# Channel mix: both squares of every pair on ScalarE, and other buffers for the last three stores of stage one

## The chip, the cores and the metric

The kernel runs on one core of one Trainium2 chip. The metric is the device time of one execution in microseconds; the time before is 2052.75 us, the median of 3 runs (2052.17 to 2054.95).

## What is computed

Three layers in a row on x of 4 x 3072 x 256 numbers (fp32). The second one is where the change lies; its `k * k` is what the change moves.

```python
def _attn_ref(x, w_r, w_i, b_r, b_i):            # a Fourier layer
    X = np.fft.rfft(x, axis=1)
    Yr = X.real @ w_r - X.imag @ w_i + b_r
    Yi = X.real @ w_i + X.imag @ w_r + b_i
    ...                                          # soft threshold of Yr and Yi at 0.01
    return np.fft.irfft(Yr + 1j * Yi, n=x.shape[1], axis=1)

def _moe_ref(x, mu_k, mu_r, w_k, w_v, w_r):      # the channel mix
    x_prev = ...                                 # x one step earlier
    xk = mu_k * x + (1.0 - mu_k) * x_prev
    xr = mu_r * x + (1.0 - mu_r) * x_prev
    k = np.maximum(xk @ w_k, 0.0)                # 256 -> 1024
    v = k * k @ w_v                              # 1024 -> 256
    return 1.0 / (1.0 + np.exp(-(xr @ w_r))) * v

def _moe2_ref(x, w_in, w_out):                   # 256 -> 2048 -> 256
    h = x @ w_in
    return h * np.tanh(softplus(h)) @ w_out
```

## The kernel before

Every fp32 operand of a matmul is split in two: a part rounded to the matmul's input type (high, `h` at the end of a name) and the rest (low, `l`). A product is three matmuls: high x high, high x low, low x high. `split` (lines 70 to 77) makes both parts: ScalarE casts, VectorE subtracts.

*Stage one*, to 329 us, is the forward transform, the mixing with `w_r` and `w_i`, and the first half of the inverse transform, in 48 units `u`. `load_A` brings a unit from DRAM into tag `A` (four buffers, called the operand ring here), `is1_ev` (lines 392 to 397) copies a result from PSUM into tag `Cs` (two buffers) with ScalarE and stores it to DRAM.

*The channel mix*, 329 to 1022 us, goes over 32 sweeps `t` of 384 columns, in a loop whose body is written out by hand: engines execute in the order in which the code issues. TensorE's order in a sweep is, for the pairs `P = 4t` to `4t + 3` (`i2` from 0 to 3): k of this pair (`emit_k`, line 745, 12 matmuls), v of the pair two before (`emit_v`, line 783, 12 matmuls), and then in pair 0 the second half of the next sweep's inverse transform (`is2`, line 466, 8 matmuls into tile `pp`), in pair 1 the gate (`emit_r`, line 722, 12 matmuls into `pp`), in pair 3 the first half of the transform for the sweep after. `pp` has one PSUM buffer for all three, v has one, k has two.

`k_ev` handles a pair's k: ScalarE's relu into `kr`, then the split for the transform's xk or xr (`then`), then the square, as `kh` and `kl` (two buffers each). Even pairs square twice on ScalarE (lines 768 and 769, rounded and whole) and subtract on VectorE (770). Odd pairs square on VectorE (765), cast on ScalarE (76) and subtract on VectorE (77).

Others that the steps name: `is2_ev` (472 to 485) empties `pp` into `yT`: ScalarE copies to `ya`, VectorE adds. `v_ev` (788 to 792) multiplies the gate with v on VectorE and so frees v's buffer; it is issued in pair 2, behind the `kl` of pair 1. `r_ev` is the gate's sigmoid. `bg` puts decoding steps of the next layer's weights in between (VectorE, lines 117 to 136, and a split). When a sweep is the first of a batch, four more matmuls come (line 440).

*The last layer*, from 1022 us, uses neither.

Of the kernel before, what the change touches and what calls it, by code (L numbers as in the profile page):

```python
# [8 lines left out]
F32 = mybir.dt.float32  # L9
# [8 lines left out]
B, S, D, FK, FF = 4, 3072, 256, 1024, 2048  # L18
N1, N2 = 96, 32
NG = 12  # L20
NU = B * NG
# [8 lines left out]
def kernel(  # L30
# [40 lines left out]
    def split(src, hi, lo, lo_eng=None, hi_eng=None):  # L71

        if hi_eng is nc.vector:
            nc.vector.tensor_copy(out=hi, in_=src)
        else:
            nc.scalar.copy(out=hi, in_=src)  # L76
        (lo_eng or nc.vector).tensor_tensor(out=lo, in0=src, in1=hi, op=ALU.subtract)  # L77
# [77 lines left out]
    p1p = p1.__enter__()  # L155
# [133 lines left out]
    def gview(scr, g):  # L289

        return scr.rearrange("s n d -> (s n) d")[256 * g:256 * (g + 1)].rearrange("(e p) d -> p e d", e=2)
# [100 lines left out]
    def is1_ev(u):  # L392
        b, g = divmod(u, NG)
        p = i1_t.pop(u)
        st = p1p.tile([128, 2, D], F32, tag="Cs", name="Cs", bufs=2)
        nc.scalar.copy(out=st, in_=p)
        nc.sync.dma_start(out=gview(scr2[b], g), in_=st)

# [203 lines left out]
    for u in range(NU + 3):  # L602
# [21 lines left out]
        if u > 2:  # L624
            is1_ev(u - 3)
# [128 lines left out]
    def k_ev(P, then):  # L754
        p = kp_t.pop(P)
        v = p[:, :, 0:TA]
        kr = pap.tile([128, 2, TA], F32, tag="kf", name="kr", bufs=2)
        nc.scalar.activation(out=kr, in_=v, func=AF.Relu)
        if then:
            then()  # L760
        kh = pap.tile([128, 2, TA], F32R, tag="kh", name="kh", bufs=2)
        kl = pap.tile([128, 2, TA], F32R, tag="kl", name="kl", bufs=2)
        if P % 2:

            nc.vector.scalar_tensor_tensor(out=kr, in0=v, scalar=0.0, in1=kr, op0=ALU.max, op1=ALU.mult)  # L765
            split(kr, kh, kl)
        else:
            nc.scalar.activation(out=kh, in_=kr, func=AF.Square)
            nc.scalar.activation(out=kr, in_=kr, func=AF.Square)
            nc.vector.tensor_tensor(out=kl, in0=kr, in1=kh, op=ALU.subtract)  # L770
        kk_t[P] = (kh, kl)
# [27 lines left out]
    for t in range(NA + 1):  # L799
# [5 lines left out]
        for i2 in range(4):  # L805
            P = 4 * t + i2
# [52 lines left out]
            if live:  # L859
                k_ev(P, then)  # L860
# [285 lines left out]
```

## Time and profile before

| | |
|---|---|
| median of 3 runs | 2052.75 us |
| the profiled execution, its span | 2050.79 us, 2049.0 us |
| TensorE busy | 1994.8 us, 97% of the span |
| VectorE, ScalarE, GpSimd busy | 1590.5, 1094.4, 29.6 us |
| stage one, 0 to 329 us: TensorE, VectorE, ScalarE busy | 304.3, 281.6, 195.5 us |
| channel mix, 329 to 1022 us: the same | 676.0, 518.9, 427.8 us |
| last layer, 1022 to 2049 us: the same | 1014.6, 790.0, 471.1 us |
| granted TensorE clock in the three stages | 0.94, 1.00, 1.00 |

Where TensorE is busy 97% of the time, the time to be had lies in its gaps, and a gap is read from the wait that ends it. Durations below are of the one profiled execution.

### The profile page before, as it was taken

To read this page: it belongs to the slowest core of one execution; us is meant where nothing else is said; L and a number is where in the kernel's file an instruction comes from. 1 tells how busy PE (TensorE), PEld (TensorE's weight loads), DVE (VectorE), ACT (ScalarE), POOL (GpSimd) and SP (SyncE) were. 2 spreads that over 40 slices of the span, in tenths; PEclk is the share of its full clock that TensorE was granted. 3 is DMA by queue.
4 is the path that set the end of the run, shared out by engine and by line. 5 is a ranking of instruction groups with operands and counts; after the bars stand their busy time and mean duration, and the time that the engine had idled before them with its cause. 6 is when DMAs were issued, how large, how long until landed. Compare 5 with 4: busy or idle time off the path is not lost.

```text
span 2049.0 us, 33355 instructions
## 1 busy us (share of the span) xinstructions
PE 1994.8 (97%) x13284; PEld 1896.1 (93%) x13284; DVE 1590.5 (78%) x2545; ACT 1094.4 (53%) x1635; POOL 29.6 (1%) x48
## 2 busy tenths in 40 slices
PE   6999998999999999999999999999999999999998
PEld 5999998999999999999979999999999999999997
DVE  5899997777777777777578777777778777787775
ACT  5666555666666666666544444444444444444443
POOL 1000000000000000000000000000000000000000
PEclk6999999999999999999999999999999999999999
DMA  8566632111211212111000000000100001010000
GB/s 254 164 190 205 182 118 75 60 55 59 65 48 57 69 48 67 59 55 48 23 32 31 22 26 27 25 29 21 32 22 29 25 21 32 22 32 21 22 11 21
DMA packets 71499, 123.17 MB, mean 60 GB/s; under 512 B 6192, under 2 KB 48432, under 8 KB 71344
## 3 DMA queue, kind: packets, MB, share of 16 engines
q1 hardware_dynamic: 66864, 105.31, 17.5%
q0 software_dynamic: 4480, 15.73, 2.0%
q8 instruction: 105, 1.72, 0.3%
q14 instruction: 50, 0.41, 0.1%
HBM read 70.69 MB, written 50.33 MB: 59 GB/s over the span
## 4 chain that ended last, share of the span: by engine, by line
PE 76%; DVE 14%; ACT 5%; issue 3%; DMA 2%; SPq 0%; ACTq 0%; DVEq 0%; POOLq 0%
PE h L970 19%; PE o L1018 17%; PE o L1019 9%; PE vp L783 8%; PE kp L745 7%; PE mxp L361 5%; PE p L970 3%; PE s2p L315 2%; PE pp L722 2%; PE pp L466 1%; DVE kl L770 1%; PE s1p L274 1%; DVE kr L765 1%; ACT kh L76 1%; DVE Dl L77 1%
## 5 line engine op out<-in xcount | busy, mean ns | idle before, releaser
L1018 PE MATMUL o<-WO,gh 128*128 128x512 f32 x1536 | 563.4, 395 | 0.0
L1019 PE MATMUL o<-WO,gl 128*128 128x256 f32 x1536 | 431.2, 281 | 0.0
L970 PE MATMUL h<-xS,WS 128*128 128x256 f32 x2208 | 351.9, 282 | 0.0
L1018 PEld LDWEIGHTS o<-WO,gh 128*128 128x128 f32 x1536 | 289.8, 189 | 43.3
L983 ACT COPY p1s<-p 128x256 f32<-128x256 f32 x184 | 68.5, 372 | 478.5 <-PE p L970 477.5
L970 PEld LDWEIGHTS h<-xS,WS 128*128 128x128 f32 x2208 | 300.6, 189 | 16.1
L1019 PEld LDWEIGHTS o<-WO,gl 128*128 128x128 f32 x1536 | 290.4, 189 | 0.2
L745 PE MATMUL kp<-xk,WK 128*128 128x384 f32 x1536 | 290.6, 337 | 0.0
L783 PE MATMUL vp<-kh,WV 128*128 128x384 f32 x1024 | 283.8, 338 | 6.3 <-DVE r L791 6.0
L745 PEld LDWEIGHTS kp<-xk,WK 128*128 128x128 f32 x1536 | 266.6, 188 | 0.1
L973 DVE TENSOR_TENSOR C<-h,p1s 128x512 f32<-128x512 f32 x184 | 127.0, 690 | 163.9 <-PE h L970 163.9
L955 DVE TENSOR_TENSOR gl<-g,gh 128x1024 fp32r<-128x1024 f32 x184 | 223.5, 1215 | 2.1 <-ACT g L952 2.1
L951 ACT ACTIVATE gh<-C 128x1024 fp32r<-128x1024 f32 x184 | 195.7, 1064 | 10.8 <-DVE C L973 10.8
L783 PEld LDWEIGHTS vp<-kh,WV 128*128 128x128 f32 x1024 | 186.4, 188 | 12.8 <-DVE r L791 12.7
L952 ACT ACTIVATE g<-C 128x1024 f32<-128x1024 f32 x184 | 193.0, 1049 | 0.0
L970 PE MATMUL h<-xS,WI 128*128 128x256 f32 x1104 | 190.2, 281 | 0.0
L973 DVE TENSOR_TENSOR C<-h,wu 128x512 f32<-128x512 f32 x368 | 187.3, 550 | 1.8 <-PE h L970 1.8
L783 PE MATMUL vp<-kl,WV 128*128 128x384 f32 x512 | 171.7, 335 | 0.0
L970 PEld LDWEIGHTS h<-xS,WI 128*128 128x128 f32 x1104 | 156.1, 189 | 0.0
L973 DVE TENSOR_TENSOR wu<-h,C 128x512 f32<-128x512 f32 x184 | 126.5, 687 | 37.5 <-PE h L970 33.6
L361 PE MATMUL mxp<-WX,Xh 128*128 128x256 f32 x752 | 138.7, 285 | 0.0
L76 ACT CAST kh<-kr 128x768 fp32r<-128x768 f32 x64 | 53.4, 835 | 154.0 <-DVE kr L765 152.7
(153 smaller groups left out, 3206.1 us busy)
## 6 DMA issues: line engine op xcount, KB each, us to landing
xs<-in_x_dram SPq DMA_DIRECT2D x32, 384.0 KB
A<-scr SPq DMA_DIRECT2D x48, 256.0 KB
scr<-Cs SPq DMA_DIRECT2D x48, 256.0 KB
D<-scr SPq DMA_DIRECT2D x32, 384.0 KB
x2d<-r POOLq DMA_DIRECT2D x32, 384.0 KB, 3.5
x<-x2d SPq DMA_DIRECT2D x24, 512.0 KB
out_dram<-ob SPq DMA_DIRECT2D x96, 128.0 KB
scr<-st SPq DMA_DIRECT2D x24, 384.0 KB
```

The source lines that it names most:

```text
L76: nc.scalar.copy(out=hi, in_=src)
L361: nc.tensor.matmul(out=p[:, e, :], lhsT=a, rhs=WX[:, dh, c, w, :], start=(i == 0), stop=(i == 11))
L745: nc.tensor.matmul(out=p[:, m, 0:TA], lhsT=WK[:, dh, w, f * 128:(f + 1) * 128], rhs=hl[:, v, dh, :], start=(i == 0), stop=(i == 5),)
L783: nc.tensor.matmul(out=p[:, o, 0:TA], lhsT=WV[:, f, w, o * 128:(o + 1) * 128], rhs=v[:, m, :], start=(f == 0 and i == 0), stop=(f == 7 and ...
L951: nc.scalar.activation(out=gh, in_=c, func=AF.Mish)
L952: nc.scalar.activation(out=g, in_=c, func=AF.Mish)
L955: nc.vector.tensor_tensor(out=gl, in0=g, in1=gh, op=ALU.subtract)
L970: nc.tensor.matmul(out=out, lhsT=a(l), rhs=xS[:, v, b, :], start=(n == 0), stop=(n == 2))
L973: nc.vector.tensor_tensor(out=out, in0=x0, in1=x1, op=ALU.add)
L983: nc.scalar.copy(out=p1s, in_=p1)
L1018: nc.tensor.matmul(out=o[m], lhsT=gh[:, m2, ms], rhs=WO[:, f], start=(f == 0), stop=False)
L1019: nc.tensor.matmul(out=o[m][:, 0, :], lhsT=gl[:, m2, ms], rhs=WO[:, f, 0, :], start=False, stop=(f == 15))
```

## The change

Odd pairs take the way of even ones: both squares on ScalarE. And the units 45, 46 and 47 of stage one copy their result into buffers of tag `A` instead of `Cs`.

```diff
     def is1_ev(u):
         b, g = divmod(u, NG)
         p = i1_t.pop(u)
-        st = p1p.tile([128, 2, D], F32, tag="Cs", name="Cs", bufs=2)
+        tag, n = ("Cs", 2) if u < NU - 3 else ("A", 4)
+        st = p1p.tile([128, 2, D], F32, tag=tag, name="Cs", bufs=n)
         nc.scalar.copy(out=st, in_=p)
         nc.sync.dma_start(out=gview(scr2[b], g), in_=st)
...
         kh = pap.tile([128, 2, TA], F32R, tag="kh", name="kh", bufs=2)
         kl = pap.tile([128, 2, TA], F32R, tag="kl", name="kl", bufs=2)
-        if P % 2:
+        if False:
 
             nc.vector.scalar_tensor_tensor(out=kr, in0=v, scalar=0.0, in1=kr, op0=ALU.max, op1=ALU.mult)
             split(kr, kh, kl)
```

The order on TensorE, GpSimd and the DMA queues is the same as before (lines behind 395 move on by one). ScalarE at the end of pair 3 and in pair 0 of a sweep (place A of the prediction), before:

```order
L76 CAST xr<-xf 128x768 [waits DVE_49]
L76 CAST kh<-kr 128x768 [waits DVE_49,PE_49]
L476 COPY yT<-yT 128x3x32 x2
L479 COPY ya<-pp 128x384 [waits PE_49]
L758 ACTIVATE kr<-kp 128x768 [waits PE_49,Activation_49]
L768 ACTIVATE kh<-kr 128x768 [waits PE_49,Activation_49]
```

The same place now:

```order
L76 CAST xr<-xf 128x768 [waits DVE_49]
L769 ACTIVATE kh<-kr 128x768 [waits PE_49,Activation_49]
L770 ACTIVATE kr<-kr 128x768 [waits Activation_49]
L477 COPY yT<-yT 128x3x32 x2
L480 COPY ya<-pp 128x384 [waits PE_49]
L759 ACTIVATE kr<-kp 128x768 [waits PE_49]
L769 ACTIVATE kh<-kr 128x768 [waits PE_49,Activation_49]
```

In front of the copies to yT stand two squares that wait for ScalarE and TensorE alone, where a cast stood that waited for VectorE.

VectorE from pair 1 to pair 2 of a sweep (place B), before:

```order
L494 TENSOR_TENSOR dl<-yT 128x768
L77 TENSOR_TENSOR Dl<-D,Dh 96x1024
L765 SCALAR_TENSOR_TENSOR kr<-kp,kr 128x768
L77 TENSOR_TENSOR kl<-kr,kh 128x768
L791 TENSOR_TENSOR r<-r,vp 128x768
L77 TENSOR_TENSOR ifh<-ift,ifh 96x4x96
```

The same place now:

```order
L495 TENSOR_TENSOR dl<-yT 128x768
L77 TENSOR_TENSOR Dl<-D,Dh 96x1024
L771 TENSOR_TENSOR kl<-kr,kh 128x768
L792 TENSOR_TENSOR r<-r,vp 128x768
L77 TENSOR_TENSOR ifh<-ift,ifh 96x4x96
```

The square between Dl and kl is gone; the product with the gate stands behind kl as before.

ScalarE at the end of stage one (the stores' copies `Cs`, then the first work of the channel mix), before:

```order
L76 CAST Yh<-yt 128x512 [waits DVE_49,PE_49,Activation_49]
L396 COPY Cs<-i1p 128x512 [waits DMAHW3_49,Activation_49]
L396 COPY Cs<-i1p 128x512 [waits DMAHW4_49,PE_49,Activation_49]
L396 COPY Cs<-i1p 128x512 [waits DMAHW5_49,PE_49,Activation_49]
L476 COPY yT<-yT 128x3x32 x2
L479 COPY ya<-pp 128x384 [waits PE_49]
```

The same place now:

```order
L76 CAST Yh<-yt 128x512 [waits DVE_49,PE_49,Activation_49]
L397 COPY Cs<-i1p 128x512
L397 COPY Cs<-i1p 128x512 [waits PE_49] x2
L477 COPY yT<-yT 128x3x32 x2
L480 COPY ya<-pp 128x384 [waits PE_49]
```

The three copies no longer wait for a store (DMAHW) to land. The first cast and subtraction of decoded weights, in the channel mix, wait for these three stores instead.

## Rows read from the trace of the kernel before

**Rows 1.** Windows, the channel mix: from:to, us, busy by engine, clock, DMA share, GB/s.

```profile
329.00:1022.00 693.00, 675.96 (x3984) 659.79 (x3984) 518.86 (x829) 427.78 (x630) 23.38 (x32) 1.00 0.18 55
```

**Rows 2.** Waits over the span: waiting engine and line, releaser: us, times, longest.

```profile
ACT kh L76 <- DVE kr L765: 152.7, 63, 3.5
...
PE pp L466 <- DVE yT L482: 9.1, 9, 3.2
...
PE vp L783 <- DVE r L791: 6.0, 13, 0.9
...
ACT Cs L396 <- DMA scr<-Cs: 2.1, 1, 2.1
```

**Rows 3.** Timeline of TensorE, the gate's blocks of sweeps 1, 29, 30: start, us.

```profile
359.78 2.27 PE L722 MATMUL pp<-xr,WR 128*128 128x384 f32 x12
...
961.63 2.27 PE L722 MATMUL pp<-xr,WR 128*128 128x384 f32 x12
...
982.46 2.27 PE L722 MATMUL pp<-xr,WR 128*128 128x384 f32 x12
```

**Rows 4.** Groups by line: busy us, mean ns of one | idle before.

```profile
L765 DVE SCALAR_TENSOR_TENSOR kr<-kp,kr 128x768 f32<-128x768 f32 x64 | 60.7, 948 | 0.0
...
L768 ACT ACTIVATE kh<-kr 128x768 fp32r<-128x768 f32 x64 | 54.2, 847 | 14.2 <-PE vp L783 11.2
L769 ACT ACTIVATE kr<-kr 128x768 f32<-128x768 f32 x64 | 54.2, 847 | 2.0
L76 ACT CAST kh<-kr 128x768 fp32r<-128x768 f32 x64 | 53.4, 835 | 154.0 <-DVE kr L765 152.7 <-PE vp L783 1.3
...
L731 ACT ACT_TABLE_LOAD x1 | 1.3, 1283 | 0.0
```

**Rows 5.** Timelines of ScalarE, VectorE, TensorE near 500 us (place A).

```profile
499.55 0.83 ACT L76 CAST xr<-xf 128x768 fp32r<-128x768 f32 x1 [0.95 <-DVE xf L502]
...
502.09 0.95 DVE L765 SCALAR_TENSOR_TENSOR kr<-kp,kr 128x768 f32<-128x768 f32 x1
504.00 0.96 DVE L77 TENSOR_TENSOR kl<-kr,kh 128x768 fp32r<-128x768 f32 x1 [0.96 <-ACT kh L76]
504.87 0.68 DVE L482 TENSOR_TENSOR yT<-ya,pp 128x128 f32<-128x128 f32 x3
...
505.70 0.33 PE L466 MATMUL pp<-ifh,Dh 96*128 96x192 f32 x1 [0.80 <-DVE yT L482]
...
506.65 2.28 PE L745 MATMUL kp<-xk,WK 128*128 128x384 f32 x12
```

**Rows 6.** Timeline of TensorE, the same place near 977 us.

```profile
976.98 0.34 PE L783 MATMUL vp<-kh,WV 128*128 128x384 f32 x1
977.31 0.33 PE L466 MATMUL pp<-ifh,Dh 96*128 96x192 f32 x1
```

**Rows 7.** Timeline near 517 us, an even pair behind its v block.

```profile
517.10 2.27 PE L745 MATMUL kp<-xk,WK 128*128 128x384 f32 x12
517.36 0.85 ACT L768 ACTIVATE kh<-kr 128x768 fp32r<-128x768 f32 x1 [0.40 <-PE vp L783]
...
519.12 0.96 DVE L770 TENSOR_TENSOR kl<-kr,kh 128x768 fp32r<-128x768 f32 x1 [1.17 <-ACT kr L769]
```

**Rows 8.** Timeline near 534 us (place B).

```profile
531.66 2.27 PE L722 MATMUL pp<-xr,WR 128*128 128x384 f32 x12
...
534.48 0.96 DVE L77 TENSOR_TENSOR kl<-kr,kh 128x768 fp32r<-128x768 f32 x1 [0.95 <-ACT kh L76]
535.36 0.95 DVE L791 TENSOR_TENSOR r<-r,vp 128x768 f32<-128x768 f32 x1
...
536.36 0.44 PE L783 MATMUL vp<-kh,WV 128*128 128x384 f32 x1 [0.34 <-DVE r L791]
```

**Rows 9.** Timelines of TensorE and ScalarE, end of stage one.

```profile
328.62 0.41 PE L466 MATMUL pp<-ifh,Dl 96*128 96x192 f32 x1
...
329.18 0.48 ACT L479 COPY ya<-pp 128x384 f32<-128x384 f32 x1
```

## The prediction

> **What bounds the kernel now.** I read the page's engine table and its 40 slices first (TensorE 97% busy, ScalarE 53%, so only TensorE's gaps are worth anything), then a table of windows by stage. The channel mix, 329 to 1022 us, is where the second edit lies: there TensorE is busy 676.0 of 693 us at a granted clock of 1.00, that is the upper of its two levels (2.4 GHz) [rows 1]. As the page counts it 17 us are idle. The waits view says who ends that idle time: VectorE's assembly of yT (9.1 us, nine waits, the longest 3.2, in the first sweep) and VectorE's product of the gate with v (6.0 us, 13 waits). The largest wait of the stage is not TensorE's: ScalarE stood 152.7 us in front of the odd pairs' cast, waiting for VectorE's square [rows 2].
>
> The view of idle time undercounts, since a matmul's modelled end overlaps the next one. So I measured by starts: the gate's matmuls begin at 359.78 us in sweep 1 and at 961.63 in sweep 29, 28 sweeps at 21.49 us; the next sweep, without decoding of weights, takes 20.83 [rows 3].
>
> **What the second edit removes and adds.** A sweep has four pairs of k blocks; pairs 1 and 3 are odd. Each of the 64 odd pairs loses VectorE's square (948 ns) and ScalarE's cast (835 ns) and gains two ScalarE squares (847 ns each) [rows 4]. VectorE loses 64 x 0.948 = 60.7 us, ScalarE gains 64 x (2 x 0.847 - 0.835) = 55.0 us. Neither sum is time by itself: ScalarE is 428 of 693 us busy in this stage and would be 483 [rows 1]. What counts is that a chain ScalarE, VectorE, ScalarE, VectorE becomes ScalarE, ScalarE, VectorE. Two places wait for that chain.
>
> Place A, the second half of the inverse transform (pair 0 of a sweep; its PSUM buffer must be emptied into yT). In the sweep near 500 us ScalarE ends the xr cast at 499.55 + 0.83 = 500.38, VectorE starts the odd square only at 502.09, behind the decode steps and xr's low part, the cast waits for it, the low part kl starts at 504.00, yT at 504.87, and TensorE goes on at 505.70 after 0.80 us idle, hence idle since 504.90 [rows 5]. With both squares on ScalarE, 0.88 apart as in an even pair, the second ends at 500.4 + 0.88 + 0.85 = 502.1. VectorE is free by then (it began the old square at 502.09), so kl starts near 502.2, 1.8 us earlier, and so does yT, whose ScalarE copies stand behind the cast or the squares: done at 503.9 instead of 505.7. TensorE wants it at 504.9 or, with a weight load ahead, 504.7. The wait goes, with some 0.8 us to spare.
>
> The same place costs a little in sweeps where no idle time is listed. In the sweep of 20.83 the last v matmul starts at 976.98 and the first one of the transform at 977.31, 0.33 apart, while the twelve matmuls of a block, 2.27 us in all [rows 3], are 0.17 apart [rows 6]. I find this extra 0.16 to 0.17 in all sweeps whose stall is not larger. It is late by the same chain, so it may go too: 30 x 0.17 = 5 us at most.
>
> Place B, the first v block of a sweep, whose PSUM buffer VectorE's product with the gate must have read. An odd pair's first ScalarE square must wait for the v block before (the high part has two buffers), then square, square, kl, product, and v may start. An even pair shows the head of this chain: the block after v starts at 517.10, the square at 517.36, kl at 519.12, 2.02 us behind [rows 7]. In the sweep near 534 the gate's block starts at 531.66; kl started at 534.48 behind VectorE's late square, the product at 535.36, and v at 536.36 after 0.34 idle [rows 8]. By the new chain kl starts at 531.66 + 2.02 = 533.68 (VectorE was idle from 533.53, and without its square earlier still), the product 0.88 later, done at 535.51. TensorE wants to start v at 536.36 - 0.34 - 0.17 = 535.85, and its weights 0.17 before that. So the wait goes too, but with only about 0.1 to 0.3 us to spare: here the change adds a wait, two ScalarE passes behind the v block instead of one. Behind the waiting square ScalarE holds the gate's sigmoid, the cast of the transform matrix and the next relu. The sigmoid needs the gate's block, which ends some 2.1 us after the square may start, and two squares take 1.73: they cost it nothing.
>
> A rule of the Trainium skill speaks against the edit: "ScalarE: Activation LUTs", section "Rules for kernel authors", gives products to VectorE, which it calls up to about three times faster per element in bf16. This trace has fp32, and its rows differ: 847 ns on ScalarE against 948 on VectorE [rows 4]. If ScalarE's pass were three VectorE passes (an estimate by that page, 2.8 us), chain B would be 4 us longer and each sweep slower by over 3 us; the rows rule that out.
>
> Activation tables: the stage loads one table, 1.28 us, in front of the first sigmoid, though squares of even pairs and sigmoids alternate after it [rows 4]. The last odd pair's squares now fall between two Mish passes, which none did before. The issue order of the changed kernel has the same three loads, so I add nothing; were two added, 2 x 1.28 = 2.6 us.
>
> **The first edit.** The last three stores of stage one take free buffers of the operand ring. It removes ScalarE's 2.1 us wait for a store to land [rows 2]. But the next thing on TensorE's path is the copy ya, which started at 329.18, when the last transform matmul, started at 328.62 and 0.41 long, had just ended at 329.03 [rows 9]. ScalarE would otherwise have stood waiting there. So I take 0; the ends are a gain of 2.1 us, if something hidden from the view hangs on it, and a loss of as much, should the first cast of the decoded weights, which now waits for these three stores, be early enough to notice; it stands behind a load and seven VectorE steps, so I don't expect that.
>
> **The sum.** Two ways. By starts: 28 x (21.49 - 20.83) = 18.5, less three sweeps with the four extra matmuls of a new batch (eight of these take 0.95 us [rows 5], so 0.5 each, 1.4 in all) = 17.1; the first sweep's 3.2 us wait shortens by the 1.8 of place A; the 0.17 of each sweep, 5 us, may go as well: 18.9 to 23.9. By waits: B is 6.0 plus 13 x 0.17 that the view doesn't count, 8.2; A without the first sweep 5.9 + 8 x 0.17 = 7.3; the steady rest 20 x 0.17 = 3.4; the first sweep 1.8; together 20.7. I take 21.5, near the middle, since B's margin is thin. Other stages are not touched, and the last one is TensorE-bound, so nothing there takes it back. The profiled execution took 2050.79 (span 2049.0 and 1.8 around it), 1.96 below the median: 2050.8 - 21.5 = 2029.3 there, 2031.2 against the median. I say 2031.
>
> **Rivals.**
> 1. *Only A goes.* Chain B is as long as TensorE's two blocks, and the two squares put in what VectorE's square took out. For it: a margin of 0.1 to 0.3 us, and semaphore times that I know only from one even pair. Against it: kl moves up by 0.8 in rows 8. The gain is 21.5 - 8.2, about 13, or 10 if the steady rest of A stays too: 2040 to 2043.
> 2. *Nothing to measure.* The waits were the visible end of another limit (PSUM's single buffer for the transform, the D loads), which then shows up at the same places. For it: the buffer for p is single and used three times a sweep. Against it: in the sweep of 20.83 all of these are there and only decoding is missing. 2050 to 2053.
> 3. *Slower: ScalarE's in-order queue.* The first square of pair 1 stands for the v block before it, and everything behind it, relu and yT copies too, slips. It decides from the point where chain B is later than it is now: now kl starts 2.8 us behind the gate's block (534.48 - 531.66), so the two squares would have to cost over 0.8 us more than in an even pair. At 1.2 us more, 31 sweeps lose 0.4 each, the 13 us that A gives, and beyond that the kernel is slower: at 2.0 more, 31 x 1.2 = 37 lost against 13 gained, 2077. Nothing in the rows gives that.
>
> **How the numbers follow.** The forecast 0.68 (2027 to 2036 by itself: all of 24 and part of the store's 2.1, down to 17); rival 1 0.16; rival 2 0.10; rival 3 0.04; the remainder 0.02 for a table load or a clash that I don't see, which leaves a gain. The range goes from 2026 (24 plus the 2.1, and the scatter of the median) to 2043, so as to hold rival 1. What a measurement of this kernel can tell from no change is about 0.2%, 4 us. Faster: forecast, rival 1 and the remainder, 0.86; within: rival 2, 0.10; slower: 0.04.
>
> **What would show it.** Right: the sweep by the gate's starts falls to 20.6 to 20.9; TensorE's waits for yT and for the gate product vanish but for the first sweep, which waits about 1.4; ScalarE's 152.7 us wait is gone and its squares wait for v blocks instead; TensorE idles less than 7 us in the stage. Wrong: TensorE still waits for the product with kl 2.6 us or more behind the gate's block (rival 1), or the sweep stays at 21.5 with another name in the waits (rival 2). A transition from stage one that is shorter by 2 us would show that the store's wait did count.

## The result and the profile after

The changed kernel takes 2022.97 us (median of 4 runs, 2022.33 to 2023.18) against 2053.32 us before in the same series, 30.3 us less: a ratio of 0.9849, 95% interval 0.9837 to 0.9862. The forecast was 2031, its range 2026 to 2043, so the direction and the mechanism came out and the size did not: the gain is 1.4 times the 21.5 us that the prediction summed up. Of the executions below, one of e1 (2174.77 us at a mean granted clock of 0.85) and one of e4 (5265.76 us) stand apart and are in no median or ratio here; e1's trace is of the former, so the starts of its gate's blocks can't be compared.

The channel mix is where it went. In the window of the stage after (329 to 994 us; columns as in [rows 1]) TensorE is busy in all but 1.3 us:

```profile
329.00:994.00 665.00, 663.67 (x3978) 662.37 (x3977) 461.27 (x763) 480.69 (x691) 23.37 (x32) 1.00 0.18 57
```

All its waits in that stage, first for TensorE and then the two longest of ScalarE, answer to [rows 2]:

```profile
PE pp L723 <- DVE yT L483: 1.3, 1, 1.3
```

```profile
ACT kh L769 <- PE vp L784: 88.9, 94, 1.3
ACT kr L759 <- PE kp L746: 40.2, 62, 3.2
```

TensorE no longer waits for yT or for the gate product in any sweep behind sweep 0's first gate. The 1.3 us that are left stand ahead of that gate and stood there before; they are not the 1.4 that the prediction left to the first sweep's transform, where no wait remains. ScalarE's 152.7 us in front of the cast are gone; what it waits for now is TensorE. ScalarE is busier (481 us, forecast 483) and VectorE less (461), and neither number is what made the time.

The gate's block of sweep 0 on TensorE's timeline, before:

```profile
335.71 2.34 PE L722 MATMUL pp<-xr,WR 128*128 128x384 f32 x12 [1.35 <-DVE yT L482]
```

The gate's blocks of sweeps 0, 1, 29 and 30 now answer to it and to [rows 3]:

```profile
336.17 2.34 PE L723 MATMUL pp<-xr,WR 128*128 128x384 f32 x12 [1.33 <-DVE yT L483]
...
356.83 2.27 PE L723 MATMUL pp<-xr,WR 128*128 128x384 f32 x12
...
934.60 2.27 PE L723 MATMUL pp<-xr,WR 128*128 128x384 f32 x12
...
955.18 2.27 PE L723 MATMUL pp<-xr,WR 128*128 128x384 f32 x12
```

From sweep 1 to 29 it is 577.77 us now, 601.85 before: 24.1 less. A sweep is 20.58 to 20.59 us, every one (21.04 with a new batch's four matmuls). Sweep 0, gate to gate, is 20.66 instead of 24.07: 3.4 less. The last two sweeps give 0.25. Together 27.7 us, which is what the two profiled executions differ by within 0.3 (2050.79 and 2023.18). The medians differ by 2.7 more; two of the experiments look for that.

Place B after, the sweep that answers to [rows 8] (all engines; start, us):

```profile
521.97 2.27 PE L723 MATMUL pp<-xr,WR 128*128 128x384 f32 x12
522.23 0.85 ACT L769 ACTIVATE kh<-kr 128x768 fp32r<-128x768 f32 x1 [1.32 <-PE vp L784]
...
523.11 0.85 ACT L770 ACTIVATE kr<-kr 128x768 f32<-128x768 f32 x1
...
523.99 0.96 DVE L771 TENSOR_TENSOR kl<-kr,kh 128x768 fp32r<-128x768 f32 x1 [0.79 <-ACT kr L770]
...
524.87 0.94 DVE L792 TENSOR_TENSOR r<-r,vp 128x768 f32<-128x768 f32 x1
...
525.98 0.19 PEld L784 LDWEIGHTS vp<-kh,WV 128*128 128x128 f32 x1
526.15 0.33 PE L784 MATMUL vp<-kh,WV 128*128 128x384 f32 x1
```

kl starts 2.02 us behind the gate's block, as the even pair had shown [rows 7]; the product ends at 525.81 and v's weight load starts at 525.98, in its normal place 0.17 ahead of the matmul. The margin is 0.17 us, between the 0.1 and 0.3 that were forecast.

Place A after, the end of yT and what waits for it, answers to [rows 5, 6]:

```profile
515.08 0.67 DVE L483 TENSOR_TENSOR yT<-ya,pp 128x128 f32<-128x128 f32 x3
...
516.72 0.34 PE L784 MATMUL vp<-kh,WV 128*128 128x384 f32 x1
516.72 0.19 PEld L467 LDWEIGHTS pp<-ifh,Dh 96*128 96x128 f32 x1
516.89 0.25 PE L467 MATMUL pp<-ifh,Dh 96*128 96x192 f32 x1
```

yT is done at 515.75, 0.97 us before the weight load, and the transform follows the last v matmul at 0.17 instead of 0.33: the small steady delay of [rows 6] is gone as well.

### The profile page after: what moved, and what is told of

The parts are those of the page before. It is cut to its first block, busy times and chain, and to the rows that moved or that the text cites. A ratio compares the mean times of both kernels' runs of the same rounds, so it can differ in the third digit from the quotient of the medians.

```text
span 2021.0 us, 33421 instructions
## 1 busy us (share of the span) xinstructions
PE 1985.3 (98%) x13284; PEld 1901.4 (94%) x13284; DVE 1533.5 (76%) x2481; ACT 1147.9 (57%) x1699; POOL 29.6 (1%) x48
## 4 chain that ended last, share of the span: by engine, by line
PE 92%; DVE 4%; DMA 2%; ACT 1%; issue 1%; SPq 0%; ACTq 0%; POOL 0%; POOLq 0%
PE h L971 19%; PE o L1019 17%; PE kp L746 13%; PE vp L784 13%; PE o L1020 9%; PE mxp L361 5%; PE pp L723 3%; PE p L971 3%; PE pp L467 3%; PE s2p L315 2%; PE s1p L274 2%; PE i1p L385 1%; DMA xs<-in_x_dram 1%; DMA A<-scr 1%; DVE Xl L77 0%
## 5 line engine op out<-in xcount | busy, mean ns | idle before, releaser
L771 DVE TENSOR_TENSOR kl<-kr,kh 128x768 fp32r<-128x768 f32 x128 | 122.9, 960 | 162.6 <-ACT kr L770 162.5
L769 ACT ACTIVATE kh<-kr 128x768 fp32r<-128x768 f32 x128 | 108.3, 846 | 88.9 <-PE vp L784 88.9
```

## The experiments

Each is an edit of the kernel before or of the changed one. Ratios are against the kernel before in the same series, with their 95% interval.

**Which of the two edits.** The second alone, `if P % 2:` made `if False:` in the kernel before:

> The second edit alone (both squares of odd pairs on ScalarE); stage one stores from its old buffers. Theory: the stores' buffers are worth nothing, so this kernel takes what the changed one takes, 2023 +- 1 us, with the gate's starts 20.59 us apart. Rival: the 2 to 3 us by which the medians differ more (30.3) than the profiled channel mix (27.7) come from the stores; then 2025 to 2026.

Measured 2024.25 us, ratio 0.9855 (0.984 to 0.987). That is as the whole change within the intervals, but too near to both forecasts to tell them apart; the other half does. The first alone, `tag, n = ("Cs", 2) if u < NU - 3 else ("A", 4)`:

> The first edit alone (the last three stores of stage one from the operand ring). Theory: 2053 +- 1 us, as before: ScalarE's 2.1 us wait for a store is gone from the waits, but ya starts when the last transform matmul ends, as before, and the gate of sweep 0 starts no earlier. Rival: 2050 to 2051, with the gate of sweep 0 some 2 us earlier.

Measured 2054.4 us against 2053.5, ratio 1.0003 (0.9994 to 1.0012): a gain of 1.2 us at most, where the rival wanted 2 to 3. ScalarE's copies at the end of stage one show why; no store is waited for, but the last copy now waits for TensorE's i1 and ya for the transform:

```profile
329.32 0.59 ACT L397 COPY Cs<-i1p 128x512 f32<-128x512 f32 x1 [0.56 <-PE i1p L385]
...
330.64 0.48 ACT L480 COPY ya<-pp 128x384 f32<-128x384 f32 x1 [0.39 <-PE pp L467]
```

So the wait of 2.1 us was cover for another, as forecast, and the squares are the whole change as far as it can be measured.

**Which of the two places.** From the kernel before, with ScalarE squaring in pair 3 alone:

```diff
-        if P % 2:
+        if P % 4 == 1:
```

> The kernel before with both squares on ScalarE in pair 3 of each sweep alone; pair 1 as before. Theory: place A and place B are separate, so A's wait goes (by starts 14.3 us with the first sweep, and 2.5 us of slow restarts, less the 1.5 of the first sweep that pair 1 causes: some 15) and B's 10 to 12 us stay: 2038 us. Rival: the two are one budget; TensorE, early from A, waits longer at B for VectorE: 2042 us or more, with waits of v for the gate product of clearly over 6.0 us in all.

Measured 2041.0 us, ratio 0.9934 (0.9921 to 0.9948). And in pair 1 alone (`if P % 4 == 3:`):

> The kernel before with both squares on ScalarE in pair 1 of each sweep alone; pair 3 as before. Theory: B's wait goes (10.4 us by starts, 2.2 of slow restarts, 1.5 in the first sweep: some 14) and A's stays: 2039 us. Rival: what B frees is waited for at A: 2044 us or more, with waits for yT of clearly over 9.1 us in all.

Measured 2039.06 us, ratio 0.9925 (0.991 to 0.994). TensorE's waits in the channel mix, of pair 3 alone and then of pair 1 alone:

```profile
PE vp L783 <- DVE r L791: 8.0, 15, 0.9
PE pp L466 <- DVE yT L482: 2.0, 2, 1.3
PE pp L722 <- DVE yT L482: 0.4, 1, 0.4
```

```profile
PE pp L466 <- DVE yT L482: 7.1, 9, 1.2
PE i1p L385 <- ACT Cs L396: 1.8, 1, 1.8
PE pp L722 <- DVE yT L482: 1.3, 1, 1.3
```

Each edit takes its own place's wait away (in e3 all but 2.0 us in and ahead of the first sweep), and the other place's stays. But the two are not independent. The gate's starts of sweeps 1 and 29, of pair 3 alone and then of pair 1 alone:

```profile
356.58 2.27 PE L722 MATMUL pp<-xr,WR 128*128 128x384 f32 x12
...
949.49 2.27 PE L722 MATMUL pp<-xr,WR 128*128 128x384 f32 x12
```

```profile
360.72 2.27 PE L722 MATMUL pp<-xr,WR 128*128 128x384 f32 x12
...
950.66 2.27 PE L722 MATMUL pp<-xr,WR 128*128 128x384 f32 x12
```

These 28 sweeps take 592.91 us with pair 3 alone, 8.9 less than before, and 589.94 with pair 1 alone, 11.9 less. Together that is 20.8 of the 24.1 that both give at once. What is missing lies at B: with A's delay gone, v starts late in 27 of the 28 sweeps instead of 22, and B costs 15.1 us instead of some 11.7. So e3 came out between its theory and its rival (2041.0, against 2038 and 2042 or more; its listed waits at B are 8.0 instead of 6.0): A's delay had hidden part of B's. The ratios, 13.5 and 15.4 us against 31 for the whole change, are too coarse to show this.

**How tight is place B.** The changed kernel with the rounded square written twice in pair 1, one ScalarE pass more, and with half of it written first:

```diff
+            if P % 4 == 1:
+                nc.scalar.activation(out=kh, in_=kr, func=AF.Square)
             nc.scalar.activation(out=kh, in_=kr, func=AF.Square)
```

> The changed kernel with one ScalarE pass more (0.88 us, the rounded square written twice) in pair 1 of each sweep. In the profile of the changed kernel the gate product ends at 525.81 and the weight load of v, which it must precede, starts at 525.98: 0.17 to spare. Theory (the chain v, square, square, kl, product, v is that close to TensorE's two blocks): the pass makes it late by 0.7 us in each of 31 sweeps, with 0.1 to 0.3 lost on restart: 25 to 31 us, 2048 to 2054. Rival (the margin is larger, as something in the chain can move up): under 15 us, below 2038.

> The changed kernel with half a ScalarE pass more (one of two column halves of the rounded square written first, about 0.5 us alone and 0.4 when it overlaps) in pair 1. Theory: late by 0.25 to 0.3 us and 0.1 to 0.3 of restart: 11 to 18 us, 2034 to 2041. Rival (a larger margin): 2023 to 2028.

Measured 2047.2 us for the whole pass (ratio 0.9967, 0.9954 to 0.998) and 2037.7 for the half (0.9918, 0.9901 to 0.9935): 24 and 15 us more than the changed kernel's median. The first is 1 us below what the theory allowed, far above the rival. Gate to gate a sweep takes 21.30 us with a pass, 0.71 more: the pass of 0.88 less the margin of 0.17. With half a pass, which puts the next square 0.55 us later, it takes 20.96 to 20.97, 0.38 more, and that is again the addition less 0.17:

```profile
442.95 2.27 PE L723 MATMUL pp<-xr,WR 128*128 128x384 f32 x12
...
463.91 2.27 PE L723 MATMUL pp<-xr,WR 128*128 128x384 f32 x12
```

From the gate of sweep 0 to that of sweep 31 the traces show 21.7 and 11.4 us more than the changed kernel's; the medians' further 2.5 to 3.4 us lie within the intervals. Now TensorE's waits in these two, whole and half:

```profile
PE vp L786 <- DVE r L794: 13.3, 31, 0.5
```

```profile
PE pp L723 <- DVE yT L483: 1.3, 1, 1.3
PE vp L786 <- DVE r L794: 0.2, 1, 0.2
```

With half a pass the matmuls' rows list 0.2 us for the place that loses 0.38 us in every sweep, and with a whole one 0.43 of 0.71. Their idle time is counted from the modelled end of the last matmul, which is 0.34 us behind its start, while the next one in time starts at 0.17 [rows 6]. The time isn't lost to the view, though: it stands in the waits of the weight loads (PEld), which have rows of their own. Half a pass in the changed kernel, and then the kernel before:

```profile
PEld vp L786 <- DVE r L794: 12.7, 30, 0.4
```

```profile
PEld vp L783 <- DVE r L791: 12.7, 22, 1.2
```

30 waits of 0.42 us are close to 0.38 in each sweep, and the changed kernel lists no such wait from 340 us to the stage's end.

**How loose is place A.** The same pass in pair 3 (`if P % 4 == 3:`):

> The changed kernel with one ScalarE pass more (0.88 us) in pair 3. In the changed kernel's profile yT is done at 515.75 us and the transform's weight load starts at 516.72: 0.97 to spare. Theory: the pass fits, 2023 to 2027, with small waits in some sweeps with much decoding. Rival (A is as tight as B): 2045 or more.

Measured 2023.3 us, ratio 0.9849 (0.9834 to 0.9864), as the changed kernel: 0.88 us fits into 0.97. A sweep takes 20.57 to 20.58 us; only sweep 0 is longer, 21.01 instead of 20.66.

**What made the long waits at A.** The kernel before with decode steps moved from pair 3 to pair 2:

```diff
-            bg((4, 1, 1, 3)[i2])
+            bg((4, 1, 3, 1)[i2])
```

> The kernel before with the three decode steps of pair 3 put into pair 2 and the one of pair 2 into pair 3; nothing else. Theory: A's long waits (0.80 idle, eight sweeps) come from decode steps that stand before VectorE's square in pair 3; they shrink to the 0.17 of the other sweeps: 5 to 8 us less, 2045 to 2048, if B does not grow. Rival (the long waits have another cause): 2053.

Measured 2046.6 us, ratio 0.9962 (0.9948 to 0.9977). The waits:

```profile
PE vp L783 <- DVE r L791: 6.0, 13, 0.8
PE pp L466 <- DVE yT L482: 2.4, 1, 2.4
PE pp L722 <- DVE yT L482: 1.3, 1, 1.3
```

Eight of nine waits for yT are gone, only the first sweep's is left, and B's are as before. Sweeps 1 to 29 take 595.62 us by the gate's starts, 6.2 less. The 0.8 us were three decode steps ahead of VectorE's square in its queue.

**Why the medians differ by more than the profiles.** In the profiles of e2 and e8 I saw something that the profile of before does not have: behind the first sweep's wait the clock is down. To test it, the squares moved in the first sweep alone (kernel before, `if P % 2 and P > 3:`), and in all but the first (changed kernel, `if P in (1, 3):`):

> The kernel before with both squares on ScalarE in the first sweep alone (pairs 1 and 3 of 128). By the profiled starts sweep 0 falls from 24.07 to 20.66 us, 3.4. In two profiles of kernels that keep the first sweep's 3.2 us wait, the granted clock falls to 0.6 to 0.7 in the 10 us behind it (355 to 365 us) and the matmuls there lose some 3 us more; in the profile of before it stays at 1.00. Theory: that fall is common, and the wait costs its length and, in most executions, the fall: 5 to 6.5 us less, 2047 to 2049. Rival (the clock has nothing to do with it): 3.4 us, 2050 to 2051.

> The changed kernel with the first sweep's pairs 1 and 3 as before. Theory: the 3.2 us wait and the fall of the clock behind it come back: 5 to 6.5 us more than the changed kernel, 2028 to 2030. Rival: 3.4 us more, 2026 to 2027.

Measured 2046.8 us against 2054.1 for the first sweep alone (ratio 0.9965, 0.9952 to 0.9977: 4.7 to 9.9 us, above the rival's 3.4), and 2029.6 for all but the first, 6.6 more than the changed kernel's median. The second is the weaker of the two: the medians are of two series, and by the ratios it is 5.1, with intervals that touch. One sweep of 32 gives a fifth to a quarter of the change. The windows 350 to 366 us, of the kernel before, of all but the first sweep, and of the changed kernel (the clock is the third number from the end):

```profile
350.00:366.00 16.00, 12.82 (x77) 12.53 (x76) 12.55 (x22) 10.29 (x16) 0.70 (x1) 1.00 0.26 77
```

```profile
350.00:366.00 16.00, 12.81 (x63) 12.52 (x62) 11.25 (x20) 7.43 (x13) 0.00 (x0) 0.79 0.18 58
```

```profile
350.00:366.00 16.00, 16.00 (x97) 16.00 (x96) 10.91 (x20) 11.94 (x17) 0.70 (x1) 1.00 0.31 93
```

The first two have the same idle time, 3.2 us; the second did 63 matmuls in these 16 us where the first did 77. On its timeline the k block behind the wait shows the lower level:

```profile
357.66 0.50 PE L467 MATMUL pp<-ifh,Dh 96*128 96x192 f32 x1 [3.19 <-DVE yT L483]
...
359.45 4.08 PE L746 MATMUL kp<-xk,WK 128*128 128x384 f32 x12
363.35 0.37 PE L784 MATMUL vp<-kh,WV 128*128 128x384 f32 x1
```

Twelve matmuls take 3.9 us to the next start instead of 2.1, and sweep 0 takes 26.74 gate to gate instead of 24.07. The kernel before's profiled execution did not have it. If most of its executions do, as e9's result suggests, its profile was 2.7 us short of what its median pays here. This is argued and not shown: the executions behind the median have no trace, and the end of stage one varies from execution to execution by as much (last section). Of the four profiles with this 2.4 to 3.2 us wait three show the fall (e2, e8, e10); those with a wait of 1.4 us or less in this place (among them e3, e4 and e11) or none (the changed kernel's, e9's) show 1.00.

**A try at the seam.** The changed kernel with sweep 1's inverse transform moved into stage one, where TensorE idles 1.8 us in front of the last i1:

```diff
+        elif k in (15, 16):
+            for m0 in (0, 2):
+                pe_half(1, k - 15, m0)
...
-    is2(1, 0, pp())
...
-                    is2_ev(t + 1, 0)
-                    is2(t + 1, 1, pp())
+                    if t:
+                        is2_ev(t + 1, 0)
+                        is2(t + 1, 1, pp())
...
-                    is2_ev(t + 1, 1)
+                    if t:
+                        is2_ev(t + 1, 1)
```

> The changed kernel, and the inverse transform of sweep 1 moved forward: its 16 matmuls go into stage one's PSUM buffers, behind the second last and the last unit's i1, where TensorE stood 1.8 us idle and where the clock falls behind the gap; sweep 0 then has no transform to wait for (1.3 us). If gaps at the seam cost their length and a fall of the clock: 2 to 4 us less than the changed kernel, 2019 to 2021. If the seam is bound by the chain of the last unit on ScalarE and VectorE, 2022 to 2024.

Measured 2023.8 us, ratio 0.9851 (0.9838 to 0.9865): no gain. Its waits from 320 us on:

```profile
PE pp L467 <- DVE yT L483: 1.4, 1, 1.4
PE kp L749 <- DVE yT L483: 1.1, 1, 1.1
PE i1p L385 <- ACT Cs L397: 0.9, 1, 0.9
PE s1p L467 <- ACT ya L480: 0.2, 1, 0.2
```

The 1.8 and 1.3 us of the changed kernel became 0.9, 0.2, 1.1 and 1.4: much the same gap in four pieces. That fits the forecast's second case, a seam held by the chain of the last unit on ScalarE and VectorE; no run tests that chain by itself. The gate of sweep 0 starts 0.8 us earlier (335.40), less than it varies between executions, that of sweep 1 0.8 later (357.59). No version here beats the changed kernel.

## Why the prediction was right in kind and too small

*Which wait ends.* Right: both places, by the chains that were worked out, B with 0.17 us to spare and A with 0.97 (forecast 0.8). e3, e4, e7 and e8 tell them apart; e5 and e6 show that B's margin is no more than that. What the prediction didn't see is that A's delay hid some 3 us of B's. As both went at once, that cost the forecast nothing.

*The sum by starts, sweeps 1 to 29.* The step that failed first is the floor. It took the sweep of 20.83 us as stall-free but for 0.17, and then only part of that, "21.5, near the middle", because B looked thin. The sweep's true length is 20.59. What 20.83 still held was 0.17 of late start and some 0.08 in the transform's eight matmuls behind it (0.95 us to the next block at a late start [rows 5]; a transform in time takes 0.87), which [rows 6] couldn't show. (Nor did all sweeps have the 0.17: in two of the three with a new batch's matmuls the transform starts in time.) So the 28 sweeps gave 24.1 where this sum had 17.1 to some 22, and the forecast, 21.5 less 1.8 for the first sweep, 19.7.

*The sum by waits.* It took the waits of the matmuls' rows and added 0.17 to each. At B that is 13 waits and 8.2 us. By the starts before, against the distances of the changed kernel, B was late in 22 of the 28 sweeps and cost some 11.7 us with its slow restarts; A cost some 12.4, where the sum had 7.3 and 3.4. So B's term was the worst, and the trace had the better number: the waits of the weight loads list 12.7 us in 22 places (shown with e6). Taking the mean of a sum by starts and one by waits pulled the better number towards the worse.

*The first sweep.* Priced at 1.8 us, the delay at place A alone. The trace had 3.4: pair 1's slow chain had also held up VectorE's queue earlier in that sweep (the xr operand started at 347.33 us, 11.6 behind the first gate, before and at 345.78, 9.6 behind it, after), and both delays reach TensorE. And then the clock, put at nothing: probably 2.7 us more. The one profile of before has no fall behind this wait. But it has one at the end of stage one, behind a wait of 1.79 us; the matmul that ends the wait, and the window around it:

```profile
325.84 0.69 PE L385 MATMUL i1p<-Yh,WC 128*128 128x512 f32 x1 [1.79 <-ACT Cs L396]
```

```profile
325.00:330.00 5.00, 4.16 (x16) 3.91 (x17) 1.00 (x3) 2.58 (x7) 0.00 (x0) 0.66 0.35 116
```

So a 3.2 us gap in a stage whose other gaps are at most 1.35 us was the place to ask what a gap costs beyond its length.

The three errors, 4.4 us in the sweeps, 1.6 and probably 2.7, all lay on one side, and the range ended at 2026, with 24 us and the stores' 2.1, so it missed by 3 us.

*The stores.* Right, 0.

*Rivals.* "Only A goes" fell with e4 to e6: B goes, though with little to spare. "Nothing to measure" and the slower one fell with the result. The sentence on the activation tables held; the changed kernel has the three loads of before. So did the rows set against the Trainium skill's rule ("ScalarE: Activation LUTs", "Rules for kernel authors") that gives products to VectorE: in this kernel's fp32 a ScalarE square is 846 to 847 ns and the VectorE pass that it replaced 948 [rows 4].

## What to carry to other kernels

When a pass moves from one engine to another, don't count busy time; follow the chain of hand-overs that the waiting engine stands behind, and ask what stands ahead of each link in its queue: an operation that fits by itself was late here because three decode steps stood ahead of it. Measure what a stage can win by the starts of equal blocks, from the shortest distance between any two of each kind, and read the waits of TensorE's weight loads beside those of its matmuls: the matmuls' rows left out nearly all of a 0.4 us delay that the weight loads' listed. A delay at one place can hide part of a delay at the next, so test each change alone and compare the sum with both. And look for a gap that stands alone in a busy stage: it may cost more than its length.

## What had not been expected of the hardware

A wait of TensorE of 2.4 to 3.2 us in sweep 0 was followed in three of four profiles by some 6 us at the lower clock level (1.2 GHz; twelve matmuls of 384 columns in 3.9 us instead of 2.1), in the fourth not at all. The end of stage one varies too: over the five profiles of kernels that leave it as before (before, e3, e4, e8, e9) the gate of sweep 0 starts between 334.4 and 338.6 us, and over all profiles the granted clock is 0.66 to 1.00 in the windows around 325 to 335 us. The three with the fall had started that gate at 337.1 us or later, the one without at 335.7; that is too few to make a rule. Why one execution gets the fall and another doesn't was not settled.
